# Loads of a cached GQA block and its parallel Mish branch, on one DMA queue and on two in turn

## The chip, the cores and the metric

The kernel runs on one core of one Trainium2 chip. The metric is the device time of one execution in microseconds (us). The kernel before was run three times: 1337.96, 1338.43 and 1340.22 us, median 1338.43.

The core has a matrix engine (PE, with its weight loads shown as PEld), a vector engine (DVE), a scalar engine (ACT, ScalarE), GpSimd (POOL) and a sync engine (SP), which here only issues transfers. Sixteen DMA engines move the data. An engine that issues transfers does so in its own order of instructions: a transfer that must wait for a buffer holds up what stands behind it on that engine. In the profile, SPq and ACTq are such issues of the sync engine and of ScalarE.

## The reference, cut to what matters

```python
x = A_x                                   # 8 x 1 x 512
xn = _layernorm(x, axis=-1)
# attention: 32 query heads, 8 key/value heads, 8192 cached keys, 128 wide
q = (xn @ wq).reshape(B, Sq, Hq, Dh).transpose(0, 2, 1, 3)
scores = einsum("bhqd,bhkd->bhqk", q, repeat(k_cache, 4)) * (Dh ** -0.5)
o = einsum("bhqk,bhkd->bhqd", softmax(scores), repeat(v_cache, 4))
A = o.transpose(0, 2, 1, 3).reshape(B, Sq, Hq * Dh) @ wo
# dense, Mish, dense; 1792 wide
h = xn @ w1 + b1
Bo = (h * tanh(softplus(h))) @ w2
return x + A + Bo
```

All is float32. Keys and values are 8 (batch) x 8 (heads) x 8192 x 128 each, 268 MB a side, and every byte is used once. The weights are some 24 MB.

## The kernel before, in words

**Units.** The work on the caches is cut into units of 2 MB: half of the keys (4096) of one batch row and one key/value head, or the same of the values. There are 8 heads x 2 halves x 8 rows = 128 units of keys and 128 of values. The host has laid the arrays out so that a unit is one contiguous block. In on-chip memory a unit is 128 partitions x 16 KB. A key unit goes in as two pieces of 8 KB a partition (`load_k`, issue at L92), a value unit as one piece of 16 KB (`load_v`, L104). Blocks of wq, wo and w1 go in as pieces of 4 KB, or 3.5 KB, a partition (`load_blocks`, L86: wq and w1 2 MB and 1.8 MB, wo 1 MB), and w2 as three loads of 4, 2 and 1 times 4 KB a partition (`load_w2`, L114).

**Buffers.** All loads use one pool of nine equal buffers (`BUFS`, `buffer` at L79). A load may go out when the matmuls that read its buffer's last content, nine loads earlier, are done. It also waits until the load eight before it has landed, because the eight completion counters of transfers are reused in turn.

**Order.** The list `items` (L473 to L495) holds the loads in the order of use, each with the work that uses it. First comes wq for two heads, then key units. From the second head on, a key unit and a value unit of the head before it alternate; the last head's value units stand alone. w1's two loads stand near the beginning, the next wq every second head, wo at the end of each head's values, and w2's three loads at the very end. The loop at L498 writes the load of the item six places ahead (`AHEAD`), then the work of the item itself, then what was put off (`late`). A scheduler behind the kernel then sets the order on each engine, and follows this one closely. Before the change, all of these loads are issued by the sync engine, in one line; ScalarE issues only x (L118) and b1 (L120).

**Work.**
- `setup` normalizes x: sums and scalings on DVE, Square (L162) and Sqrt (L166) on ScalarE; then a transpose on PE (L175).
- `project` (L194 to L219) makes the queries of one head for all eight rows.
- `scores` (L235) multiplies a key unit by the queries in 16 matmuls. The scores of all eight rows of a head are collected in PSUM; at the last row, DVE takes the maximum (L245).
- `maximum` and `weights` (L254 to L284): the maximum passes through two small PE transposes (L255, L268). Then ScalarE computes two exponentials over 128 x 1024 (L276), one for each half of the keys, and DVE transposes them (L277).
- `values` (L301) multiplies a value unit by the weights in 16 matmuls; every second unit, DVE gathers the row's output (L310, L312), and PE merges it (L325).
- `outputs` (L349) multiplies a head's output by wo and adds it to `acc`. `mish` (L366 to L410) is the first dense layer and the activation, near the beginning; `down` (L416) is the second, at the very end. L510 adds the two results, and L511 stores 64 KB.

Of the kernel before, what the change touches and what calls it, by code (L numbers as in the profile page):

```python
# [28 lines left out]
BW = 1024  # L29
# [27 lines left out]
def kernel(  # L57
# [12 lines left out]
    nc = tc.nc  # L70
# [5 lines left out]
    psum = ctx.enter_context(tc.tile_pool(name="psum", bufs=1, space=PSUM))  # L76


    def buffer():  # L79
        return kv.tile([P, G * BW], F32, name="kv")  # L80

    def load_blocks(src, lo, n):

        _, rows, width = src.shape
        t = buffer()[:rows, : n * width].rearrange("p (j f) -> p j f", j=n)
        nc.sync.dma_start(t, src[lo : lo + n].rearrange("j p f -> p j f"))  # L86
        return t

    def load_k(n, b, s):
        lo = ((b * HKV + n) * NH + s) * G  # L90
        t = buffer().rearrange("p (j f) -> p j f", j=G // KA)
        nc.sync.dma_start(  # L92
            t,
            kT[lo : lo + G]
            .rearrange("(j a) p f -> j (a p f)", a=KA)
            .rearrange("j (p f) -> p j f", p=P),
        )
        return t

    def load_v(n, b, s):  # L100

        lo = ((b * HKV + n) * NH + s) * G
        t = buffer()
        nc.sync.dma_start(  # L104
            t, v[lo : lo + G].rearrange("j p f -> (j p f)").rearrange("(p f) -> p f", p=P)
        )
        return t

    w2_rows = w2.rearrange("j p f -> (j p) f").rearrange("(q i) f -> q (i f)", i=W2R)

    def load_w2(lo, hi):

        t = buffer()[:, : (hi - lo) * BW]
        nc.sync.dma_start(t, w2_rows[:, lo * BW : hi * BW])  # L114
        return t

    x_sb = const.tile([B, D], F32, name="x_sb")
# [294 lines left out]
    def down(lo, hi, w):  # L412
        for j in range(2 * lo, 2 * hi):
            for g in range(G):
                at = (j - 2 * lo) * D + g * P
                nc.tensor.matmul(  # L416
                    H[Q * g : Q * g + B, :P],
                    aT[:, j, :B],
                    w[:, at : at + P],
                    start=(j == 0),  # L420
                    stop=(j == 2 * W2R - 1),
                )
# [7 lines left out]
    def wq_item(i):  # L430
        def f(t):
            project(2 * i, t)
            project(2 * i + 1, t)

        return lambda: load_blocks(wq, i * CC, CC), f
# [37 lines left out]
    for i in range(len(k_units) + PU):  # L473

        if i % (2 * PU) == PU + PU // 2 and i < len(k_units) - PU:
            items.append(wq_item(i // (2 * PU) + 1))
        if i == 4:
            for c in range(2):
                items.append((lambda c=c: load_blocks(w1, c * CC, CC), w1_work))
        if i < len(k_units):  # L480
            u = k_units[i]
            items.append((lambda u=u: load_k(*u), k_work(*u)))
        if i >= PU:
            u = v_units[i - PU]
            items.append((lambda u=u: load_v(*u), v_work(*u)))
            if (i + 1) % PU == 0:
                n = u[0]
                items.append((lambda n=n: load_blocks(wo, n * 2, 2), wo_work(n)))
    for lo, hi in ((0, 4), (4, 6), (6, 7)):
        items.append(  # L490
            (
                lambda lo=lo, hi=hi: load_w2(lo, hi),
                lambda t, lo=lo, hi=hi: down(lo, hi, t),
            )
        )  # L495
# [54 lines left out]
```

## Time and profile before

| What | Value |
|---|---|
| median of three runs | 1338.43 us |
| the profiled execution | 1339.18 us, its span 1337.2 us |
| PE busy | 933.4 us, 70% of the span |
| ScalarE busy | 23.7 us, 2% |
| bytes moved | 561.80 MB, 420 GB/s over the span |
| idle before L235 (scores), ended mostly by a landing key unit | 181.4 us |
| idle before L301 (values), ended by a landing value unit | 54.8 us |
| mean granted PE clock | 0.856 of full speed |

A row of the groups names line, engine, operation, what it writes and reads, and a count; "busy" is the time of all of the group, and "idle before" the time that its engine stood still just ahead of it, with what ended most of that. A row of the timeline has start, duration, engine, line and operation; instructions of one kind that follow each other are one row. A row of a DMA queue has packets, megabytes and the time that its packets took, as a share of the time of all 16 DMA engines. The number behind a DMA issue is the median time from issue to landing; it holds the time behind other transfers too. A row of the windows has the busy time of each engine in that stretch, then the granted PE clock, the mean busy share of the 16 DMA engines and the rate in GB/s.

### The profile page before, as it was taken

The page shows a single profiled execution, that of the slowest core. Times are in us where ns is not written, and L with a number is a line of the kernel's source. Part 1 is how long each engine was busy: PE and PEld are TensorE (multiplying, and loading weights), DVE is VectorE, ACT ScalarE, POOL GpSimd, SP SyncE. Part 2 cuts the span into 40 slices and gives each one's busy share as a digit, 9 for nine tenths or more (in the row PEclk, how much of TensorE's full clock was granted, in tenths as well). Part 3 has the DMA queues.
Part 4 walks back from the last instruction along what each step waited for, and adds up shares of the span by engine and source line. Part 5 has one row for each costly group of instructions (what it writes and reads, how often), then busy time and mean ns, then how long its engine had stood idle before and what let it go on. Part 6 is the DMA issues. An engine that isn't in the chain of part 4 may idle for free.

```text
span 1337.2 us, 11010 instructions
## 1 busy us (share of the span) xinstructions
PE 933.4 (70%) x4948; PEld 270.6 (20%) x4948; DVE 178.6 (13%) x443; ACT 23.7 (2%) x39; POOL 3.5 (0%) x10
## 2 busy tenths in 40 slices
PE   6676777667756767768666777767776776776565
PEld 2122221122111212212121221212211121211112
DVE  2302010110102001020010201102010020100311
ACT  1000000000000000000000000000000000000000
POOL 1000000000000000000000000000000000000000
PEclk9898878888898988888898788787889878889877
DMA  9999999999999999999999999999999999999997
GB/s 385 420 421 427 423 423 423 425 424 424 426 424 423 425 424 423 423 422 426 424 424 425 424 423 422 425 423 423 424 426 425 425 423 424 424 426 425 427 427 307
DMA packets 59239, 561.80 MB, mean 420 GB/s; under 512 B 4396, under 2 KB 4528, under 8 KB 9784
## 3 DMA queue, kind: packets, MB, share of 16 engines
q1 hardware_dynamic: 59168, 561.07, 100.0%
q8 instruction: 39, 0.64, 0.2%
q14 instruction: 8, 0.07, 0.0%
q10 hardware_dynamic: 24, 0.02, 0.0%
HBM read 561.01 MB, written 0.07 MB: 420 GB/s over the span
## 4 chain that ended last, share of the span: by engine, by line
DMA 83%; PE 12%; SPq 2%; DVE 2%; issue 0%; ACT 0%; DVEq 0%; ACTq 0%
DMA kv<-in_kT 61%; DMA kv<-in_v 20%; PE s L235 7%; DMA kv<-in_w 3%; PE o L301 3%; SPq L104 2%; DVE pt L277 1%; SPq L92 1%; PE m L349 0%; PE h L416 0%; PE h L194 0%; DVE os L312 0%; PE m L288 0%; DVE os L310 0%; PE h L210 0%
## 5 line engine op out<-in xcount | busy, mean ns | idle before, releaser
L235 PE MATMUL s<-kv,qT 128*64 128x512 f32 x2048 | 597.1, 737 | 181.4 <-DMA kv<-in_kT 179.8
L301 PE MATMUL o<-kv,pt 128*16 128x512 f32 x2048 | 266.7, 627 | 54.8 <-DMA kv<-in_v 54.8
L235 PEld LDWEIGHTS s<-kv,qT 128*64 128x64 f32 x2048 | 167.3, 167 | 567.1 <-issue 330.8
L310 DVE TENSOR_SCALAR os<-o,isel 128x128 f32<-128x128 f32 x64 | 22.4, 351 | 774.7 <-PE o L301 774.7
L301 PEld LDWEIGHTS o<-kv,pt 128*16 128x16 f32 x2048 | 54.7, 113 | 244.0 <-DMA kv<-in_v 141.0
L325 PE MATMUL m<-hsel,os 128*128 128x4 f32 x128 | 24.9, 265 | 99.3 <-DVE os L312 99.3
L312 DVE SCALAR_TENSOR_TENSOR os<-o,isel,os 128x128 f32<-128x128 f32 x192 | 67.1, 350 | 6.3
L245 DVE TENSOR_REDUCE nm<-s 128x1 f32<-128x1024 f32 x16 | 19.6, 1224 | 277.2 <-PE s L235 277.2
L325 PEld LDWEIGHTS m<-hsel,os 128*128 128x128 f32 x128 | 19.3, 190 | 155.8 <-DVE os L312 155.8
L276 ACT ACTIVATE e<-s,nmx 128x1024 f32<-128x1024 f32 x16 | 17.7, 1109 | 1185.3 <-DVE nmx L270 1185.3
L277 DVE STREAM_TRANSPOSE pt<-e 128x1024 f32<-128x1024 f32 x16 | 30.8, 1965 | 1.4 <-ACT e L276 1.3
L288 PE MATMUL m<-lsel,ones 128*128 128x32 f32 x16 | 4.9, 396 | 31.1 <-DVE lsel L284 31.1
L194 PE MATMUL h<-kv,xnT 128*8 128x128 f32 x256 | 13.3, 376 | 5.7 <-DVE qT L219 3.1
L349 PE MATMUL m<-kv,oT 128*8 128x128 f32 x256 | 14.3, 398 | 3.0 <-DVE r L290 2.7
L288 PEld LDWEIGHTS m<-lsel,ones 128*128 128x128 f32 x16 | 3.8, 297 | 32.6 <-DVE lsel L284 31.8
L194 PEld LDWEIGHTS h<-kv,xnT 128*8 128x8 f32 x256 | 7.8, 114 | 9.4 <-DVE qT L219 4.7
L349 PEld LDWEIGHTS m<-kv,oT 128*8 128x8 f32 x256 | 8.2, 121 | 6.7 <-DVE r L290 3.5
L210 PE MATMUL h<-ident,qs 128*128 128x128 f32 x16 | 5.5, 448 | 4.8 <-DVE qs L204 4.8
L416 PE MATMUL h<-kv,aT 128*8 128x128 f32 x112 | 5.5, 387 | 2.1 <-DMA kv<-in_w 2.1
L371 PE MATMUL h<-kv,xnT 128*8 128x448 f32 x32 | 4.1, 632 | 3.7 <-DMA kv<-in_w 3.7
L175 PE MATMUL m<-ident,xc 8*128 8x8 f32 x4 | 0.6, 247 | 8.2 <-DVE xc L173 8.2
L204 DVE TENSOR_SCALAR qs<-h 128x128 f32<-128x128 f32 x16 | 3.9, 285 | 17.6 <-PE h L194 17.6
(72 smaller groups left out, 65.0 us busy)
## 6 DMA issues: line engine op xcount, KB each, us to landing
kv<-in_kT SPq DMA_DIRECT2D x128, 2048.0 KB, 37.0
kv<-in_v SPq DMA_DIRECT2D x128, 2048.0 KB, 38.7
kv<-in_wq SPq DMA_DIRECT2D x4, 2048.0 KB, 37.1
kv<-in_wo SPq DMA_DIRECT2D x8, 1024.0 KB, 34.9
kv<-in_w SPq DMA_DIRECT2D x2, 1792.0 KB, 30.8
kv<-in_w SPq DMA_DIRECT2D x1, 2048.0 KB
kv<-in_w SPq DMA_DIRECT2D x1, 1024.0 KB, 34.3
kv<-in_w SPq DMA_DIRECT2D x1, 512.0 KB
```

The costliest lines, as they stand in the source:

```text
L92: nc.sync.dma_start(t, kT[lo : lo + G] .rearrange("(j a) p f -> j (a p f)", a=KA) .rearrange("j (p f) -> p j f", p=P),)
L104: nc.sync.dma_start(t, v[lo : lo + G].rearrange("j p f -> (j p f)").rearrange("(p f) -> p f", p=P))
L194: nc.tensor.matmul(H[Q * h : Q * h + B, 384:512], xnT[:, c, :], w[:, c, lo : lo + DH], start=(c == 0), stop=(c == CC - 1),)
L235: nc.tensor.matmul(S[s][WK * j : WK * (j + 1), c * 512 : (c + 1) * 512], qT[n % QBUFS][:, w : w + WK], k[:, j, at : at + 512], start=(b == ...
L245: nc.vector.tensor_reduce(NM[n][:, s : s + 1], S[s], axis=AX.X, op=ALU.max, negate=True)
L276: nc.scalar.activation(e[:, s], S[s], AF.Exp, bias=nmx, accum_out=l[:, s : s + 1])
L277: nc.vector.transpose(pt[:, s].rearrange("p (m t r) -> p t m r", m=m, t=TG), e[:, s].rearrange("p (t q m) -> p t m q", t=TG, m=m),)
L301: nc.tensor.matmul(o[Q * c : Q * c + W4 * REP, :], PT[n][:, s, W4 * R * j + b : W4 * R * (j + 1) : B], vt[:, 512 * j : 512 * (j + 1)], sta ...
L310: nc.vector.tensor_scalar(os, o[:, :DH], isel[:, 0:1], None, op0=ALU.mult)
L312: nc.vector.scalar_tensor_tensor(os, o[:, DH * i : DH * (i + 1)], isel[:, i : i + 1], os, op0=ALU.mult, op1=ALU.add,)
L325: nc.tensor.matmul(M[:, 168 + b * REP : 168 + (b + 1) * REP], OS.pop((n, b)), hsel, start=True, stop=True)
L349: nc.tensor.matmul(M[Q * g : Q * g + B, 256:384], oT[n][:, h, :], w[:, h // 2, h % 2 * D + g * P : h % 2 * D + (g + 1) * P], start=(h == 0 ...
```

## The change

The four helpers that issue a load call a new function `transfer` instead of the sync engine's `dma_start`. It swaps the two entries of a list at each call and issues on the first: the first load goes to ScalarE, the second to the sync engine, and so on in turn, for units and weights alike. The order of the items, the buffers, the sizes, and all computation stay as they are. x and b1 are still issued by ScalarE, ahead of the others, and the result by the sync engine. In the changed kernel all loads carry one line number, L87, and later lines stand seven further down.

```diff
+    queues = [nc.sync, nc.scalar]
+
     def buffer():
         return kv.tile([P, G * BW], F32, name="kv")
 
+    def transfer(t, src):
+
+        queues.reverse()
+        queues[0].dma_start(t, src)
+
     def load_blocks(src, lo, n):
 
         _, rows, width = src.shape
         t = buffer()[:rows, : n * width].rearrange("p (j f) -> p j f", j=n)
-        nc.sync.dma_start(t, src[lo : lo + n].rearrange("j p f -> p j f"))
+        transfer(t, src[lo : lo + n].rearrange("j p f -> p j f"))
         return t
...
     def load_k(n, b, s):
...
-        nc.sync.dma_start(
+        transfer(
...
     def load_v(n, b, s):
...
-        nc.sync.dma_start(
+        transfer(
...
     def load_w2(lo, hi):
 
         t = buffer()[:, : (hi - lo) * BW]
-        nc.sync.dma_start(t, w2_rows[:, lo * BW : hi * BW])
+        transfer(t, w2_rows[:, lo * BW : hi * BW])
         return t
```

## The prediction

> **What bounds the kernel now.** The page comes first, from the top: busy shares, the slices, the DMA queues, the chain, the costliest groups, the issues.
>
> ```profile
> span 1337.2 us, 11010 instructions
> ...
> PE 933.4 (70%) x4948; PEld 270.6 (20%) x4948; DVE 178.6 (13%) x443; ACT 23.7 (2%) x39; POOL 3.5 (0%) x10
> ...
> DMA  9999999999999999999999999999999999999997
> GB/s 385 420 421 427 423 423 423 425 424 424 426 424 423 425 424 423 423 422 426 424 424 425 424 423 422 425 423 423 424 426 425 425 423 424 424 426 425 427 427 307
> DMA packets 59239, 561.80 MB, mean 420 GB/s; under 512 B 4396, under 2 KB 4528, under 8 KB 9784
> ...
> q1 hardware_dynamic: 59168, 561.07, 100.0%
> q8 instruction: 39, 0.64, 0.2%
> ...
> q10 hardware_dynamic: 24, 0.02, 0.0%
> ...
> DMA 83%; PE 12%; SPq 2%; DVE 2%; issue 0%; ACT 0%; DVEq 0%; ACTq 0%
> ...
> kv<-in_kT SPq DMA_DIRECT2D x128, 2048.0 KB, 37.0
> kv<-in_v SPq DMA_DIRECT2D x128, 2048.0 KB, 38.7
> ```
>
> No compute engine is full (PE 70%), but the DMA line is 9 in 39 of 40 slices and the rate hardly moves: 420 to 427 GB/s between a first slice of 385 and a last one of 307. The sync engine's queue q1 alone fills the time of 16 engines (100.0%). The chain agrees: 83% DMA. A 2 MB load passes in 2.097 MB / 424 GB/s = 4.95 us but lands 37.0 us after its issue, so some 7.5 loads stand in the queue at any time, of nine buffers. The DMA engines are never short of work; what counts is their rate while full, and the two ends. ScalarE's own queue exists already: q10, which carries x and b1.
>
> Next, the stretches by window: one of values alone, then single microseconds at the end.
>
> ```profile
> 1260.00:1320.00 60.00, 37.18 (x216) 7.49 (x208) 8.41 (x24) 0.00 (x0) 0.00 (x0) 0.74 1.01 427
> ```
>
> ```profile
> 1322.00:1323.00 1.00, 1.00 (x12) 0.13 (x4) 0.00 (x0) 0.00 (x0) 0.00 (x0) 1.00 1.09 451
> ...
> 1327.00:1328.00 1.00, 0.00 (x0) 0.00 (x0) 0.00 (x0) 0.00 (x0) 0.00 (x0) 0.50 0.50 209
> ...
> 1331.00:1332.00 1.00, 1.00 (x25) 0.72 (x20) 0.00 (x0) 0.00 (x0) 0.00 (x0) 0.50 0.22 86
> 1332.00:1333.00 1.00, 1.00 (x26) 0.78 (x20) 0.00 (x0) 0.00 (x0) 0.00 (x0) 0.50 0.00 0
> ```
>
> The last columns are granted clock, DMA share and GB/s. Up to 1323 us all engines are full; by 1327 only half of them still work, and the last load is in by about 1332.
>
> **The change part by part.** Of 273 loads, 137 go to ScalarE's queue and 136 stay with the sync engine. Bytes, packets, buffers and matmuls are the same.
>
> *The rate with two queues.* This decides, and no stretch of the trace has two busy load queues. What a packet costs beside its bytes comes from two windows with different packet sizes, units' keys (8 KB packets) and values (16 KB).
>
> ```profile
> DMA packets 1740, 13.47 MB, mean 421 GB/s; under 512 B 97, under 2 KB 97, under 8 KB 97
> ```
>
> ```profile
> DMA packets 1811, 24.71 MB, mean 426 GB/s; under 512 B 189, under 2 KB 189, under 8 KB 339
> ```
>
> The first is 48 to 80 us (32 us x 16 = 512 engine-us), the second 1262 to 1320 (928). Solving 512 = 13.47a + 1740b and 928 = 24.71a + 1811b gives a = 36.96 us per MB (27.06 B/ns an engine) and b = 8.1 ns a packet. So a 16 KB packet takes 0.614 us, one of 8 KB 0.311, one of 4 KB 0.159. Over 59239 / 16 = 3702 packets an engine, b is worth 30 us. If a second queue fills this gap, the gain is at most 30 us; if every change of queue costs a second b, 30 us are lost. The only packets that share an engine with q1 in full flight are instruction fetches of 16 KB on q8, one in each of these half-microsecond windows, among keys (57 us) and among values (1256 us):
>
> ```profile
> q8 instruction: 1, 0.02, 12.8%
> ```
>
> ```profile
> q8 instruction: 1, 0.02, 13.4%
> ```
>
> 12.8% of 16 x 0.5 us is 1.02 us, 13.4% is 1.07: against 0.614 alone, so the engine does change between queues while such a packet is under way. Own time plus one neighbour would be 0.614 + 0.311 = 0.93 among keys (0.10 over) and 0.614 + 0.614 = 1.23 among values (0.16 under). An inserted packet thus costs between 0.16 less and 0.10 more than taking turns; the loss, on half of 3702 packets, could be as much as 185 us. Zero lies between, and I take zero: 0 us, with -30 and +30 as the ends that carry weight (the row nearest to a packet's cost is b) and +185 as the outer one.
>
> *The start.* In the changed program's order ScalarE has x, b1, then the load of wq, a table load and Square, the load of the second key unit, Sqrt, and further loads.
>
> ```profile
> 0.73 0.62 ACTq L118 DMA_DIRECT2D x_sb<-in_x  x1
> 0.74 0.42 SPq L86 DMA_DIRECT2D kv<-in_wq  x1
> ...
> 1.22 2.19 SPq L92 DMA_DIRECT2D kv<-in_kT  x4
> 1.39 0.26 ACTq L120 DMA_DIRECT2D b_sb<-in_b  x1
> ...
> 9.03 1.90 PE L194 MATMUL h<-kv,xnT 128*8 128x128 f32 x32 [0.28 <-DVE xnT L178]
> ```
>
> wq's issue moves from 0.74 to about 1.65, behind b1, and its 32 packets of 4 KB an engine now alternate with 8 KB packets of keys: 32 x (0.159 + 0.311) = 15.0 us, landing near 17 us. PE first uses wq at 9.03 and then waits on DVE, not on it; so PE starts 8 us late. The nine empty buffers hide this: 9 x 4.95 = 44.6 us of loads go out before any buffer must come back, and the first comes back near 24 us instead of 16. Cost 0; without that cover, 8 us. One issue costs 2.19 / 4 = 0.55 us, on ScalarE 137 x 0.55 = 75 us beside 23.7 us of busy time in 1337: room enough.
>
> *The loads behind the exponentials.* In ScalarE's order the two activations of L276 stand between loads; a load behind them waits until the last key unit of a head is through the maximum.
>
> ```profile
> 418.55 5.33 PE L235 MATMUL s<-kv,qT 128*64 128x512 f32 x16 [3.03 <-DMA kv<-in_kT]
> ...
> 423.91 1.68 SPq L92 DMA_DIRECT2D kv<-in_kT  x1
> ...
> 429.09 1.11 ACT L276 ACTIVATE e<-s,nmx 128x1024 f32<-128x1024 f32 x1
> ```
>
> At the third head the buffer came free at 423.88 and the load was issued at once; behind the second exponential it leaves at 430.2, 6.3 us later. Behind that load wait ScalarE's further loads; the sync engine's go on. At that point two or three loads of ScalarE's queue and three or four of the other are outstanding, at least 5 x 4.95 = 25 us of work, so the DMA engines do not notice: 0. Uncovered it would be 8 x 6.3 = 50 us. In reverse, the exponentials wait for no load: the loads ahead of them in ScalarE's order need buffers that come free before the last key unit is done.
>
> *Unequal turns.* Where keys and values sit on different queues, values move 16 KB a turn and keys 8. Values run ahead, their queue empties, and keys then have the engines alone. Buffers are still reused in order of use, so one queue always has work: 0.
>
> *The end.* ScalarE's queue ends with the last value unit, w2's first piece (2 MB) and its third (0.5); the other with the value unit before, wo (1 MB) and w2's second piece (1 MB). PE's order is unchanged: wo's outputs (L349), then w2 (L416).
>
> ```profile
> 1321.22 1.93 PE L301 MATMUL o<-kv,pt 128*16 128x512 f32 x16 [1.36 <-DMA kv<-in_v]
> ...
> 1325.44 1.06 PE L349 MATMUL m<-kv,oT 128*8 128x128 f32 x32 [0.28 <-DVE oT L330]
> ...
> 1328.62 5.50 PE L416 MATMUL h<-kv,aT 128*8 128x128 f32 x112 [2.12 <-DMA kv<-in_w]
> 1334.20 0.29 DVE L510 TENSOR_TENSOR res<-h,acc 128x128 f32<-128x128 f32 x1 [7.35 <-PE h L416]
> ```
>
> Before, from the last value's landing (1321.22): wo 16 x 0.159 = 2.5 us, the first piece 8 x 0.614 = 4.9, together 7.4, which is just where L416 starts (1328.62); then 2.5 and 1.3 more, to 1332.4, where the windows fall to zero. With turns of one packet the last two value units land together, at the same 1321.2, since the same bytes follow. Then eight packets of the first piece alternate with eight of wo's: 8 x (0.614 + 0.159) = 6.2; the other eight of wo with the third piece: 8 x 0.318 = 2.5; last the second piece, 2.5. So wo lands at 1321.2 + 8.7 = 1329.9, 6 us later than before, and PE stands behind it although w2's first piece is there. L349 to about 1331.0, L416 for 5.50 more (the second piece, at 1332.4, is in before its turn): 1336.5 instead of 1334.1, **+2.4 us**. The ends: 2 us less if the wait lets L416 run at the 0.27 us a matmul of a full clock instead of 0.42, and 0 if turns are larger (a rival below).
>
> **Sum**: 0 + 0 + 0 + 0 + 2.4. The profiled execution took 1339.18 us, 2.0 around its span; it is 0.75 over the median of the runs, 1338.43. So 1341.6 against itself, and 1340.8 against the median.
>
> **The rivals.**
> 1. *The second queue fills the gap between packets.* For it: the gap is there (b = 8.1 ns) and the insertion among values was 0.16 us cheap. Against it: q1 always had the next packet ready, 7.5 loads deep, so the gap may lie in the data path that both queues share. All of it: 1340.8 - 30 = 1311; half: 1326. The Trainium skill's page "DMA: Bandwidth & Descriptors", section "Where 436 GB/s comes from", puts the ceiling of the ports at 435.2 GB/s, by which 561.80 MB would need 1291 us, an estimate; the trace's 427 lies below it, and 1/a, 433, too.
> 2. *Slower: a change of queue costs time in each engine.* Place: every packet, as the queues alternate. For it: 0.10 us over among keys. Against it: 0.16 under among values. A second b a packet gives 1340.8 + 30 = 1371; from 0.1 ns a packet on, the sum passes +0.2%.
> 3. *Slower: the loads behind the exponentials run the engines dry.* It needs both queues empty, so an issue held back for over some 25 us against the 6.3 worked out; half the price is 1340.8 + 25 = 1366. The landing time of 37.0 us speaks against it.
> 4. *Turns of many packets.* If an engine takes a load's whole share before it changes queue, loads land nearly in the old order: wo first and the end is as before, 1338.4; w2's first piece first, and wo lands at 7.4 instead of 8.7, L416 ends 1.1 later, 1339.5. The Trainium skill, same page, section "Queues, rings and completion order", has an engine drain a packet of some 9 to 17 descriptors from one queue before it switches. The q8 rows speak against it: a single 16 KB packet was stretched while it was under way.
>
> That the change does nothing at all (all loads on one queue) is excluded: q10 carries ScalarE's transfers already.
>
> **How the numbers follow.** Forecast 0.43 (1338.8 to 1343), first rival 0.17 (1311 to 1335), second 0.20 (1343 to 1371 and above), third 0.08, fourth 0.12. About 0.2%, 2.7 us, is what a measurement of this kernel can tell from no change: 1335.8 to 1341.1. Faster 0.17 (first rival). Same 0.40: the fourth and 0.28 of the forecast. Slower 0.43: the second, the third and 0.15 of the forecast. A range from 1325 to 1362 leaves out about half of the first rival's chance (its larger part of the gap) and a third of the second's and third's, some 0.18.
>
> **What would show it.** Two load queues with about half of the bytes each; GB/s of 421 to 427 in the middle slices (433 means the first rival, under 420 the second); wq used first near 17 us instead of 9; the load behind the exponentials issued some 6 us after its buffer; DMA share still 1.01 there (a dip: the third); and at the end wo's outputs close to w2's, with L510 about 15 us after the last value unit instead of 13. The forecast falls if the middle slices differ by more than 1 GB/s, since 0.2% of 424 is 0.85.

## The result, and the profile after

The changed kernel takes 1341.26 us (median), the kernel before 1338.59 in the same runs: a ratio of 1.0019, 95% interval 1.0011 to 1.0027. That is 2.7 us more (1.5 to 3.6), just about what a measurement tells from no change. One of the changed kernel's 14 runs took 2761.63 us, for a reason that is not known, and is left out of the ratio and of this median (1341.48 with it).

The page of the changed kernel, to be read against the lines of before:

```profile
span 1340.1 us, 11019 instructions
...
DMA  9999999999999999999999999999999999999996
GB/s 385 419 422 424 426 421 424 422 425 425 426 424 420 427 423 423 424 423 425 425 426 427 419 425 422 423 426 422 424 425 424 424 424 427 424 423 424 428 427 269
...
q10 hardware_dynamic: 29608, 281.31, 50.0%
q1 hardware_dynamic: 29584, 279.78, 49.8%
...
L242 PE MATMUL s<-kv,qT 128*64 128x512 f32 x2048 | 603.2, 730 | 307.3 <-DMA kv<-in_kT 303.7
...
kv<-in_kT SPq DMA_DIRECT2D x64, 2048.0 KB, 34.1
kv<-in_kT ACTq DMA_DIRECT2D x64, 2048.0 KB, 38.5
```

The loads are split in half between q10 (ScalarE) and q1 (the sync engine), and the rate has not changed: 419 to 428 GB/s where it was 420 to 427. Only the last slice differs, 269 against 307. Meanwhile PE's idle time ahead of the scores (L235 before, L242 now) has grown from 181.4 to 307.3 us. This is a large number that costs nothing: the DMA engines set the pace, and PE is merely made to wait elsewhere. The first experiment below has 312.7 us of it in the time of before. The same stretches by window, first of before, then of after:

```profile
400.00:600.00 200.00, 141.81 (x732) 40.78 (x728) 29.84 (x73) 4.60 (x8) 0.00 (x0) 0.83 1.01 424
```

```profile
48.00:80.00 32.00, 21.95 (x96) 6.18 (x96) 11.59 (x16) 0.58 (x1) 0.00 (x0) 0.89 1.02 422
...
400.00:600.00 200.00, 140.21 (x762) 40.26 (x765) 25.59 (x67) 2.30 (x4) 0.00 (x0) 0.85 1.01 423
...
1262.00:1320.00 58.00, 40.35 (x274) 10.69 (x278) 12.55 (x30) 0.59 (x2) 0.00 (x0) 0.77 1.01 426
```

422 among keys was 421 before, 426 among values was 426. A difference of 1 GB/s all along would be worth 3 us, so the rates alone do not settle where the time went. The timeline of the end shows a difference:

```profile
1318.15 3.64 PE L308 MATMUL o<-kv,pt 128*16 128x512 f32 x32 [0.69 <-DMA kv<-in_v]
...
1324.78 1.93 PE L308 MATMUL o<-kv,pt 128*16 128x512 f32 x16 [2.67 <-DMA kv<-in_v]
...
1329.00 1.19 PE L356 MATMUL m<-kv,oT 128*8 128x128 f32 x32 [0.28 <-DVE oT L337]
...
1331.22 5.85 PE L423 MATMUL h<-kv,aT 128*8 128x128 f32 x112 [1.03 <-DMA kv<-in_w]
1337.15 0.29 DVE L517 TENSOR_TENSOR res<-h,acc 128x128 f32<-128x128 f32 x1 [6.62 <-PE h L423]
```

```profile
1327.00:1328.00 1.00, 0.00 (x0) 0.00 (x0) 0.89 (x4) 0.00 (x0) 0.00 (x0) 1.00 0.54 229
...
1331.00:1332.00 1.00, 0.78 (x16) 0.59 (x20) 0.00 (x0) 0.00 (x0) 0.00 (x0) 0.50 0.28 111
1332.00:1333.00 1.00, 1.00 (x28) 0.74 (x20) 0.00 (x0) 0.00 (x0) 0.00 (x0) 0.50 0.00 0
```

The last byte is in at the same moment as before, by 1332 us. But the last value unit is used at 1324.78 instead of 1321.22, w2's first piece at 1331.22 instead of 1328.62, and the final addition stands at 1337.15 instead of 1334.20: 2.95 us later, all of the growth of the span (1337.2 to 1340.1). Of this, 2.60 us are the later start of L423; in the other 0.35 it ran longer, 5.85 us instead of 5.50.

### The profile page after: what moved, and what is told of

Its sections match the earlier page's. It is cut to its first block, busy times and chain, and to the rows that moved or that the text cites. A ratio compares the mean times of both kernels' runs of the same rounds, so it can differ in the third digit from the quotient of the medians.

```text
span 1340.1 us, 11019 instructions
## 1 busy us (share of the span) xinstructions
PE 920.3 (69%) x4948; PEld 267.1 (20%) x4948; DVE 179.1 (13%) x443; ACT 23.8 (2%) x39; POOL 3.5 (0%) x10
## 4 chain that ended last, share of the span: by engine, by line
DMA 78%; PE 17%; another core or an unknown queue 4%; DVE 1%; issue 0%; ACTq 0%; ACT 0%; SPq 0%
DMA kv<-in_kT 62%; DMA kv<-in_v 12%; PE s L242 10%; PE o L308 5%; DMA kv<-in_w 2%; DMA kv<-in_wq 1%; PE h L201 1%; PE h L423 0%; PE m L356 0%; PE m L332 0%; PE h L217 0%; DVE pt L284 0%; PE m L295 0%; DVE os L317 0%
## 5 line engine op out<-in xcount | busy, mean ns | idle before, releaser
L242 PE MATMUL s<-kv,qT 128*64 128x512 f32 x2048 | 603.2, 730 | 307.3 <-DMA kv<-in_kT 303.7
L242 PEld LDWEIGHTS s<-kv,qT 128*64 128x64 f32 x2048 | 166.4, 166 | 711.4 <-DMA kv<-in_kT 369.6
L356 PE MATMUL m<-kv,oT 128*8 128x128 f32 x256 | 8.9, 275 | 0.3 <-DVE oT L337 0.3
L226 DVE COPY qT<-h 64x32 f32<-64x32 f32 x32 | 5.0, 208 | 15.1 <-PE h L217 15.0
L423 PE MATMUL h<-kv,aT 128*8 128x128 f32 x112 | 5.9, 406 | 1.0 <-DMA kv<-in_w 1.0
L297 DVE RECIPROCAL r<-m 128x32 f32<-128x32 f32 x8 | 2.9, 358 | 27.1 <-PE m L295 27.1
L423 PEld LDWEIGHTS h<-kv,aT 128*8 128x8 f32 x112 | 4.1, 132 | 2.9 <-DMA kv<-in_w 1.4
```

The costliest lines, as they stand in the source:

```text
L226: nc.vector.tensor_copy(t[half * a : half * (a + 1), lo : lo + R : B, :], H[half * a : half * (a + 1), k * P : (k + 1) * P].rearrange("p ( ...
L242: nc.tensor.matmul(S[s][WK * j : WK * (j + 1), c * 512 : (c + 1) * 512], qT[n % QBUFS][:, w : w + WK], k[:, j, at : at + 512], start=(b == ...
L356: nc.tensor.matmul(M[Q * g : Q * g + B, 256:384], oT[n][:, h, :], w[:, h // 2, h % 2 * D + g * P : h % 2 * D + (g + 1) * P], start=(h == 0 ...
L423: nc.tensor.matmul(H[Q * g : Q * g + B, :P], aT[:, j, :B], w[:, at : at + P], start=(j == 0), stop=(j == 2 * W2R - 1),)
```

## The experiments

**Theory**: the loss is at the end alone. Engines take one packet from each queue in turn, and so the loads that PE needs first share the engines with loads that it needs later. **Rivals**: two queues change the rate; the late wq, or the loads held behind the exponentials, cost time. All kernels were compared with the kernel before on the same chip.

**1. Turns everywhere but at the end.** The edit of the changed kernel:

```diff
+    count = [0]
+
     def transfer(t, src):
-
+        count[0] += 1
         queues.reverse()
-        queues[0].dma_start(t, src)
+        q = nc.sync if count[0] > 273 - 12 else queues[0]
+        q.dma_start(t, src)
```

> The changed kernel, but its last 12 loads (the last eight value units, wo, w2's three pieces) all go to the sync engine's queue; the 261 loads ahead still take turns. Theory (all of the loss is at the end, where two queues in turn bring the last value unit, wo and w2's first piece in later than one queue does): the loss goes, 1338.3 to 1339.3 us. Rival (the loss comes from the middle or the start: rate of two queues, late wq, loads behind the exponentials): no change against the changed kernel, 1341 to 1342.

Measured: 1338.68 us, ratio 0.9999 (0.9990 to 1.0008). The loss is gone, though start and middle still use two queues: by the interval, these cost between -1.3 and +1.1 us. The end of its timeline:

```profile
1321.08 3.20 PE L311 MATMUL o<-kv,pt 128*16 128x512 f32 x16 [2.98 <-DMA kv<-in_v]
...
1326.57 1.06 PE L359 MATMUL m<-kv,oT 128*8 128x128 f32 x32 [0.28 <-DVE oT L340]
...
1328.52 4.83 PE L426 MATMUL h<-kv,aT 128*8 128x128 f32 x112 [0.89 <-DMA kv<-in_w]
1333.43 0.29 DVE L520 TENSOR_TENSOR res<-h,acc 128x128 f32<-128x128 f32 x1 [5.44 <-PE h L426]
```

The last value unit at 1321.08 and w2 at 1328.52 are back where they were before the change (1321.22 and 1328.62).

**2. Turns at the end alone.** The condition of the first experiment turned round (`count[0] <= 273 - 20` goes to the sync engine), so that only the last 20 loads take turns.

> The kernel before, but its last 20 loads take turns on the two queues, w2's first piece on ScalarE's as in the changed kernel; the 253 loads ahead stay on the sync engine's queue. Theory (the end alone): 1340.8 to 1342. Rival (start or middle): as before, 1338.3 to 1339.0. Half and half, some 1340, if both have a share.

Measured: 1340.38 us, ratio 1.0012 (1.0003 to 1.0021). So the end alone makes the kernel slower, by 1.8 us. That is below the theory's range (1340.8 to 1342) and above the 1340 of half and half; but as start and middle cost nothing that could be measured in the first experiment, the end is the only part with a loss. The rest of the 2.7 us is within the intervals, and the end does not look the same in the two kernels. This is it here (the profiled execution, 1341.92, is the slowest of this kernel's):

```profile
1320.49 5.86 PE L311 MATMUL o<-kv,pt 128*16 128x512 f32 x32 [2.41 <-DMA kv<-in_v]
...
1329.50 1.90 PE L359 MATMUL m<-kv,oT 128*8 128x128 f32 x32 [1.13 <-DMA kv<-in_wo]
1331.16 5.25 PE L426 MATMUL h<-kv,aT 128*8 128x128 f32 x112
...
1336.49 0.29 DVE L520 TENSOR_TENSOR res<-h,acc 128x128 f32<-128x128 f32 x1 [4.74 <-PE h L426]
```

Here the last two value units come as a pair (32 matmuls in one row), L359 waits for wo, and L426 follows at once, without a wait: w2's first piece is there already.

**3. The turns exchanged.** `queues = [nc.scalar, nc.sync]`, so that wq is the sync engine's.

> The changed kernel with the turns exchanged: the first load, wq, goes to the sync engine's queue, the key unit after it to ScalarE's; at the end the value unit before the last, wo and w2's second piece are ScalarE's. Theory (end alone, start hidden): wq is first used some microseconds earlier than at 19.95, the time stays at 1340.8 to 1342.2. Rival (the late wq costs time): 1338.6 to 1339.5, less by up to the 11 us that PE waited.

Measured: 1340.70 us, ratio 1.0015 (1.0006 to 1.0024). PE's first use of wq, in the changed kernel and in this one:

```profile
19.95 1.89 PE L201 MATMUL h<-kv,xnT 128*8 128x128 f32 x32 [11.20 <-DMA kv<-in_wq]
```

```profile
13.22 1.90 PE L201 MATMUL h<-kv,xnT 128*8 128x128 f32 x32 [4.46 <-DMA kv<-in_wq]
```

PE starts 6.7 us earlier, and the median is 0.6 us lower, with intervals that overlap. In the first experiment wq went through ScalarE too, at no loss. The late start is hidden. At the end, the last value unit and w2's first piece are both late here too (1321.22 and 1328.62 before):

```profile
1323.31 1.93 PE L308 MATMUL o<-kv,pt 128*16 128x512 f32 x16 [0.55 <-DMA kv<-in_v]
...
1330.37 4.75 PE L423 MATMUL h<-kv,aT 128*8 128x128 f32 x112 [1.76 <-DMA kv<-in_w]
```

**4. and 5. ScalarE held on purpose.** Behind each head's exponentials stand further activations (28, then 72 of them), and ScalarE's next loads are kept behind these:

```diff
         queues.reverse()
-        queues[0].dma_start(t, src)
+        if held and queues[0] is nc.scalar:
+            with tc.issue_after(held[0]):
+                queues[0].dma_start(t, src)
+        else:
+            queues[0].dma_start(t, src)
+
+    held = []
...
+        junk = work.tile([P, 512], mybir.dt.bfloat16, name="junk", bufs=1)
+        for _ in range(28):
+            hold = nc.scalar.activation(junk, e[:, 0, :512], AF.Exp)
+        held[:] = [hold.ins]
```

> The changed kernel with 28 further activations of 128 x 512 behind each head's exponentials (8 heads, some 0.63 us each, 17.6 us a head, results not used), and ScalarE's next loads behind them. So a load there is held back by some 6.3 + 17.6 = 24 us. Theory (25 us of outstanding work cover it): 1341 to 1343, DMA share still 1.01 at the heads' ends. Rival (such a hold runs the DMA engines dry): up to 8 x 17.6 = 141 us more, 1360 to 1482.

Measured with 28: 1342.44 us, ratio 1.0027 (1.0015 to 1.0039); its interval overlaps that of the changed kernel. One head's hold, from its timeline, and the windows behind it:

```profile
771.40 18.49 ACT L296 ACTIVATE junk<-e 128x512 bf16<-128x512 f32 x28
```

```profile
780.00:790.00 10.00, 9.32 (x48) 2.73 (x48) 1.70 (x5) 9.45 (x15) 0.00 (x0) 1.00 1.00 417
790.00:800.00 10.00, 0.00 (x0) 0.00 (x0) 0.00 (x0) 0.00 (x0) 0.00 (x0) 0.72 1.02 429
```

PE then has nothing to do for all of 790 to 800 us (0.00 busy), since the next unit comes through ScalarE; yet the DMA share is 1.00 to 1.02, and so the time hardly moves. The last head is different: there the share falls to 0.91 from 1260 to 1270 us (372 GB/s), a loss of some 1.3 us.

> As the run with 28 activations behind each head's exponentials, but 72 (45 us a head): a load behind them is held back by some 51 us. Theory (what is outstanding in both queues covers a hold, and no more): 25 us of cover would leave 26 us a head uncovered, 8 x 26 = 210 us, so 1550; with a cover of 40 us, 1430. DMA share well under 1 behind each head's end. Rival (holds on ScalarE never matter, the other queue carries on): 1341 to 1344.

Measured with 72, in a single run: 1504.47 us, 163 over the changed kernel, 20.4 a head. The page's DMA line, the first hold, and the windows around its end:

```profile
DMA  9999599967999689996999939999399995999947
```

```profile
120.17 47.58 ACT L296 ACTIVATE junk<-e 128x512 bf16<-128x512 f32 x72
```

```profile
140.00:150.00 10.00, 1.60 (x8) 0.29 (x4) 0.00 (x0) 9.50 (x16) 0.00 (x0) 0.83 1.01 418
150.00:155.00 5.00, 0.00 (x0) 0.00 (x0) 0.00 (x0) 4.78 (x8) 0.00 (x0) 0.50 0.28 116
155.00:160.00 5.00, 0.00 (x0) 0.00 (x0) 0.00 (x0) 4.75 (x9) 0.00 (x0) 0.50 0.00 0
...
165.00:170.00 5.00, 0.00 (x0) 0.00 (x0) 0.00 (x0) 2.62 (x5) 0.00 (x0) 0.50 0.37 95
```

The DMA engines stay full until about 151 us, 31 us after the exponentials' end at 120.2, and then fall dry until ScalarE issues again at 167 us. Over the eight heads, the packet records show the engines dry (fewer than eight of 16 at work) from 24 to 35 us after the start of the hold. The other queue did not carry on: in the timeline the sync engine issues nothing between 139 and 178 us. Buffers come free in the order of use, and the next unit in that order was one of ScalarE's. So a hold is free, or nearly so, while the outstanding loads last, and is paid in full after that: by the packet records, the idle time of the DMA engines during the eight holds adds up to 157 us of the 163.

**6. Longer key packets, one queue.** This measures the disputed cost of a packet by itself. The host lays a key unit out so that a partition's 16 KB are one piece:

```diff
...
-            kT[lo : lo + G]
-            .rearrange("(j a) p f -> j (a p f)", a=KA)
-            .rearrange("j (p f) -> p j f", p=P),
...
+        nc.sync.dma_start(t, kT[(b * HKV + n) * NH + s])
...
```

> The kernel before (one queue), with the host laying a key unit out so that a partition's 16 KB are one piece: key loads have 8 packets an engine instead of 16. Theory (a packet costs 8.1 ns beside its bytes, in the engine itself): 128 x 8 x 8.1 ns = 8.3 us less, 1330.3 (1329.3 to 1331.3). Rival (the 8.1 ns are an effect of the stretches compared, not of the packets): 1338 to 1339.

Measured: 1328.96 us, ratio 0.9925 (0.9912 to 0.9937), about 10.0 us less (8.4 to 11.8). The packets of the page:

```profile
DMA packets 42855, 561.80 MB, mean 423 GB/s; under 512 B 4396, under 2 KB 4528, under 8 KB 9784
```

16384 fewer (before it was 59239), 1024 an engine: 9.8 ns a packet (8.2 to 11.5), a little more than the 8.1 expected, so that the time lies just below the range given. The new layout also changes the order of addresses in memory; the two were not separated.

**7. The same, two queues in turn.**

> The changed kernel (two queues in turn) with the key units laid out in 16 KB packets as well. Theory (the second queue gives nothing in the middle, and costs 1.5 to 3 us at the end): 1331.8 to 1333.5, 1.5 to 3 over the one-queue kernel with the same packets. Rival (two queues hide part of the cost of a packet): under that kernel's time plus 1.

Measured: 1330.17 us, ratio 0.9937 (0.9924 to 0.9951), 1.2 over the one-queue kernel with the same packets. That lies between theory and rival, and the two intervals overlap. The slices do not separate the two either (425 to 429 GB/s from the second to the last but one, with one queue 423 to 430), and at the end PE again stands at wo:

```profile
1319.69 1.90 PE L350 MATMUL m<-kv,oT 128*8 128x128 f32 x32 [3.11 <-DMA kv<-in_wo]
1321.35 3.74 PE L417 MATMUL h<-kv,aT 128*8 128x128 f32 x112
```

In that execution L417 then ran in 3.74 us, where it took 5.85 in the changed kernel, which gives some of the wait back.

**8. Long packets for the weights too, one queue.** wq, wo and w1 are laid out in the same way, 16, 8 and 14 KB a partition in one piece; `load_blocks` issues one such piece.

> The kernel before (one queue) with key units and also wq, wo and w1 laid out as one piece a partition (16, 8 and 14 KB): 3328 packets less beside those of the keys. Theory (8.1 ns a packet): 3328 / 16 x 8.1 ns = 1.7 us under the kernel with long key packets alone, about 1328.6. Rival: the weights' shorter packets cost nothing, the same as that kernel.

Measured: 1327.29 us, ratio 0.9911 (0.9898 to 0.9925). That is 1.7 us under the sixth run, as expected (3328 packets, 8 ns each), though the intervals overlap. It is the fastest version, 11.9 us under the kernel before on the same chip, with one queue.

## Why the prediction was right, point by point

**The rate: right.** Zero was taken between -30 and +30 us, and 424 GB/s stayed 423 to 425. Both rivals on it fall: neither is the gap between packets filled nor does a change of queue cost. The tightest bound is the first experiment's, at most 1.3 us either way where half of the gap was worth 15 us and a second one 30. The sixth run shows that the gap is real, 9.8 ns a packet, so the second queue had something to fill and did not. The Trainium skill, page "DMA: Bandwidth & Descriptors", section "Issuing engines are not separate DMA queues", says that issuing from several engines saves only the issuing time; the trace agrees, 423 against 424 GB/s.

**Turns of one packet: right.** In the changed kernel, from 602 to 607 us, keys come through ScalarE's queue and values through the other:

```profile
q1 hardware_dynamic: 96, 1.38, 64.8%
q10 hardware_dynamic: 100, 0.76, 36.5%
```

The numbers of packets are nearly equal, the bytes nearly 2 to 1. The records do not name the engine, but one that starts where another ends can be taken as the next on the same engine. Followed in this way in that stretch (S16 is 16 KB of the sync engine's queue, A8 is 8 KB of ScalarE's), they give:

```
S16 A8 S16 A8 S16 A8 S16 A8 S16 A8 S16 A8 S16 A8
```

So the fourth rival, turns of many packets, falls. The Trainium skill's turn of some 9 to 17 descriptors (the same page, "Queues, rings and completion order") is not what this trace shows: here a turn is one record of 8 or 16 KB.

**The start: right in price, short in size.** The late wq cost nothing that could be measured, but it was first used at 19.95 us, not near 17. The packet records show why: ScalarE issued the load at 1.66, but its first 4 KB packet starts at 5.53, after some ten key packets of 8 KB on each engine, and its last one ends at 19.20. The turns themselves took 13.7 us, where 15.0 were worked out; the sum had left out the wait ahead of them. Why ScalarE's first load starts so late (at 5.81 in the third experiment, there with keys) stays open.

**The loads behind the exponentials: right, with one size off.** The held load of the same head, in the changed kernel:

```profile
433.60 3.65 PE L242 MATMUL s<-kv,qT 128*64 128x512 f32 x16 [1.65 <-DMA kv<-in_kT]
...
441.46 1.11 ACT L283 ACTIVATE e<-s,nmx 128x1024 f32<-128x1024 f32 x1 [164.91 <-DVE nmx L277]
441.62 0.37 ACTq L87 DMA_DIRECT2D kv<-in_kT  x1
```

Its buffer came free at 437.25, and it left at 441.62: 4.4 us later, not 6.3. It left 0.16 us after the first exponential's start, so it does not wait for the end of the two. In the fifth experiment, too, the load left at 167.18, before the last activation's end at 167.75. The cover was put at 25 us or more; the fifth experiment shows 24 to 35, and 31 at the first head. So the third rival is a real mechanism, which holds of 6.3 us do not reach.

**The end: right in size, in part by luck, and half right in place.** 2.4 us were forecast, the profile has 2.95. The step that failed is "the last two value units land together": in the changed kernel the row at 1318.15 holds two units, the second from about 1320, and the last one follows only at 1324.78. By the packet records the sync engine's queue was ahead: its wo took turns with the last value unit, and w2's second piece with the first. So PE waited for the last value unit and for w2's first piece instead of wo: the sum went by a load that PE did not wait for, and that its size came out is in part luck. In the second experiment the units do land together, and there the forecast fits: wo used at 1329.50 (forecast 1329.9), L426's end at 1336.41 (1336.5). Which load is late differs with how the two queues stand to each other when the end comes; some load was late in each. The four kernels with turns to the end and nothing held (the changed one and experiments 2, 3 and 7) were 1.2 to 2.7 us slower than their one-queue counterparts, the 1.2 (experiment 7) within the intervals.

What set the queues' relation at the end was not varied by itself, and stays open.

## What to carry to other kernels

Where the DMA engines are full, a second queue has nothing to give: look at the bytes and at the number of packets instead (longer packets brought 12 us here). A second queue does change the order in which loads land, and that counts wherever the order is tuned, above all at the end: keep the last loads on one queue, in the order of use. A compute engine that issues loads may be held for as long as the loads already out last (24 us or more here, with nine buffers), and PE's idle time says nothing as long as the DMA share stays at its full value.

## What the runs showed of the hardware that was not expected

- Two queues share an engine by packets, not by bytes, as the prediction took it without a trace to show it: 16 KB packets got 1.38 MB where 8 KB packets got 0.76.
- PE's work in the middle ran some 13 us behind that of before (third head's first exponential at 441.46, before at 427.99), with no trace of it in the time: the first experiment has it at 442.65 and takes as long as before. That the nine buffers took it up is likely, but was not tested.
- At 1327 us only about half of the DMA engines were at work, at 1331 about a quarter (shares of 0.54 and 0.28; before 0.50 and 0.22), with two queues as with one. That some engines are slower over the whole run would explain it, but was not tested.
